# Linear attention and a gated block on one core: matmuls whose results are not read, loads moved between periods, a sum moved to PSUM, and another order of the last output steps

## The chip, the core and the metric

The kernel runs on one core of a Trainium2 chip. The metric is the device time of one execution in microseconds (us). The engines are TensorE (PE in the profile; PEld is its weight load), VectorE (DVE), ScalarE (ACT), GpSimd (POOL) and SyncE (SP), whose queue issues every DMA here. SBUF is the on-chip memory, PSUM the memory that matmuls write.

## The reference

Attention over 4 batches, 8 heads, 768 steps, head dimension 48 keeps a 48 x 48 state for each head; its result, 4 x 768 x 384, goes through a gated block with width 1024.

```python
for t in range(S):                       # attention
    cur = einsum('bhd,bhe->bhde', u * k[t], v[t])
    y[t] = einsum('bhd,bhde->bhe', r[t], state + cur)
    state = w * state + einsum('bhd,bhe->bhde', k[t], v[t])

h = maximum(x @ w_in, 0)                 # x: y with the heads side by side
u, v = h[..., :512], h[..., 512:]
v_n = (v - mean(v)) / sqrt(var(v) + 1e-6)
v_s = einsum('ts,bsd->btd', w_spatial, v_n) + b_spatial[:, None]
out = (u * v_s) @ w_out
```

## The kernel before

The attention works in 24 chunks of 128 steps (6 for each batch), the block behind it in steps of matmuls. Matmul operands are split in a high part (rounded) and a low part (the rest), and each product is three matmuls (`mm3`, L392 to L394).

A loop over `i` from -1 to 23 writes the program, and every engine does its instructions in the order written. One pass, a period, has: the results of chunk `i` (`g2`, L336, then `fin`: ScalarE casts them to `xh`, L366); the first products of chunk `i+1` (`g1`: L287 the scores, L296 the state's update); for the first seven chunks `fin_low`, where TensorE subtracts `xh` from the results in PSUM (L376) and ScalarE copies the rest to `xl` (L377); then `mid(i+1)`: VectorE merges the scores (L310), ScalarE copies the state into two block matrices (L303, L304), and VectorE makes the next state, `t1 + ub_` (L325) times the decay `w128` (L326). After that SP issues the loads of chunk `i+3` (L91 `rk`, L95 `rkv`), and chunk `i+2` is prepared (`prep`): `scale` (L248 on GpSimd, L249 on VectorE), two products with `r` and one with `k` on GpSimd (L254, L255, L258), a sum on VectorE (L261) and the diagonal on GpSimd (L270). Between the parts stand pieces of splitting the weights (`pour`: L183 to L203 for the input and output weights; L214 to L219 for the first three pieces of the spatial weights, where TensorE copies a piece to PSUM, L214, ScalarE makes the high part, L215, TensorE subtracts it, L218, and ScalarE copies the low part, L219; L172 and L173 for the other nine) and the block's steps: `moe_v` (L392 to L394 into L406, statistics L413 to L430, norm L436, L438, L443), `moe_u` (L462 to L468), `moe_sp` (L392 to L394, then L479 adds the bias on VectorE, L480 multiplies with `u` on GpSimd, and a step later `split` makes `gt`, L172 and L173) and `moe_out` (L392 to L394 with `wo_h` and `wo_l`, copy L492 to `ob`, DMA L493). `ob` has two buffers. `moe_*` steps write to `pm`, a pool of four PSUM banks that the splits use too.

The loads of the weights stand at the end of a period: six pieces of the spatial weights and the bias after period 0, four pieces of the output weights after period 2, two more spatial pieces after period 3.

Of the kernel before, what the change touches and what calls it, by code (L numbers as in the profile page):

```python
# [7 lines left out]
F32 = mybir.dt.float32  # L8
# [3 lines left out]
ALU = mybir.AluOpType  # L12
AX = mybir.AxisListType

B, H, S, D = 4, 8, 768, 48
# [3 lines left out]
P = 128  # L19
# [4 lines left out]
NP = H // 2  # L24
NK = DM // P
NS = S // P
ND = DH // P
TH = S // 2
# [8 lines left out]
def fused_kernel(ctx, tc, rkT, rkvN, wT, uB, w_in, w_sp, b_sp, w_out, out):  # L37
# [4 lines left out]
    KPOOL, DACT, VPOOL = 8, 0, 1  # L42
    XPE, SPE = 7, 3
    SIX, LAST = 6, 1
    FIRST = [0, 1, 2, 2, 5, 10]
    POUR = [(3, 4), (2, 4), (6, 4), (1, 4), (5, 4), (1, 3), (1, 5), (0, 12), (1, 13), (0, 8)]
    const = ctx.enter_context(tc.tile_pool(name="const", bufs=1))
# [23 lines left out]
    def raw_out(k):  # L71
        t = sm.tile([P, 2 * DM], U32, name="raw", tag="gt", bufs=5)
        raws["out", k] = t.rearrange("p (n k) -> p n k", k=2)
        src = w_out[k * P:(k + 1) * P, :]
        nc.sync.dma_start(out=raws["out", k], in_=src.bitcast(U32).rearrange("p (n k) -> p n k", k=2))
# [133 lines left out]
    def sp_pieces(t, j):  # L209
        def f():  # L210
            if t * NS + j < SPE:
                hi, lo = (w[:, j, t * TH:(t + 1) * TH] for w in (ws_h, ws_l))
                pm = ps_m.tile([P, 512], F32, name="pm")[:, 0:TH]
                nc.tensor.matmul(pm, eye, raws["sp", t, j], start=True, stop=False)  # L214
                nc.scalar.copy(hi, raws["sp", t, j])  # L215

                def rest():
                    nc.tensor.matmul(pm, neg, hi, start=False, stop=True)  # L218
                    nc.scalar.copy(lo, pm)  # L219

                rests.append(rest)
                if len(rests) > 1:
                    rests.pop(0)()
                if j == NS - 1 or t * NS + j == SPE - 1:
                    rests.pop(0)()
                return
            split(ws_h[:, j, t * TH:(t + 1) * TH], ws_l[:, j, t * TH:(t + 1) * TH], raws["sp", t, j])
            if t and j + 2 < NS:
                raw_sp(t, j + 2)
        return [f]  # L230
# [45 lines left out]

    SUBS = ((0, 64, 0), (1, 0, 64))

    def g1(m):
        t = at[m]  # L280
        ps = ps_a.tile([P, 2, 512], F32, name="ps")
        t["ps"] = ps
        for p in range(NP):
            for j in range(2):
                for z, s0, t0 in SUBS:
                    hd = slice(64 * j, 64 * j + 64)
                    nc.tensor.matmul(ps[s0:s0 + 64, j, p * HC:(p + 1) * HC], t["k"][hd, p, s0:s0 + 64],  # L287
                                     t["r"][hd, p, t0:t0 + 64], start=True, stop=True, skip_group_check=True)
        for p in range(NP):
            for j in range(2):  # L290
                for z, s0, t0 in SUBS:
                    if z == 1 and m % NC == NC - 1:
                        continue
                    h = 2 * p + j
                    e0 = 0 if j == 0 else 16
                    nc.tensor.matmul(ps[64 * j:64 * j + 64, s0 // 64, 256 + p * D:256 + (p + 1) * D],  # L296
                                     t["kn"][s0:s0 + 64, h * D:h * D + 64], t["v"][s0:s0 + 64, h, e0:e0 + D],
                                     start=True, stop=True, skip_group_check=True)
# [7 lines left out]
    def mid(m):  # L306
        t, c = at[m], m % NC
        ps = t["ps"]
        ua, ub_ = (ps[:, i, 256:256 + NP * D].rearrange("p (n e) -> p n e", n=NP) for i in (1, 0))
        nc.vector.copy_predicated(out=t["a"], mask=mask_u.unsqueeze(1).unsqueeze(1).to_broadcast([P, 2, NP, HC]),  # L310
                                  data=ps[:, :, 0:256].rearrange("s j (p t) -> s j p t", p=NP))
        if c == 0:
            block(sblk[1], ua)
            t1 = ua
        else:
            block(sblk[0], st["s"])
            t1 = sm.tile([P, NP, D], F32, name="t1", bufs=1)
            nc.vector.tensor_tensor(out=t1, in0=st["s"], in1=ua, op=ALU.add)
            block(sblk[1], t1)
        if c < NC - 1:  # L320
            if c == 0:
                t1 = sm.tile([P, NP, D], F32, name="t1", bufs=1)
                nc.vector.tensor_copy(out=t1, in_=ua)
            s2 = sm.tile([P, NP, D], F32, name="s2")
            nc.vector.tensor_tensor(out=s2, in0=t1, in1=ub_, op=ALU.add)  # L325
            nc.vector.tensor_tensor(out=s2, in0=s2, in1=w128.unsqueeze(2).to_broadcast([P, NP, D]), op=ALU.mult)  # L326
            st["s"] = s2

    def g2(m):
# [61 lines left out]
    def mm3(o, lh, ll, rh, rl, first, last):  # L391
        nc.tensor.matmul(o, lh, rh, start=first, stop=False)  # L392
        nc.tensor.matmul(o, lh, rl, start=False, stop=False)  # L393
        nc.tensor.matmul(o, ll, rh, start=False, stop=last)  # L394
# [76 lines left out]
    def moe_sp(b, t, d):  # L471
        ds_ = slice(d * P, (d + 1) * P)
        ts_ = slice(t * TH, (t + 1) * TH)
        pm = ps_m.tile([P, 512], F32, name="pm")
        for s, vn in enumerate(vst[b]):
            mm3(pm[:, 0:TH], vn[:, 0, ds_], vn[:, 1, ds_], ws_h[:, s, ts_], ws_l[:, s, ts_], s == 0, s == NS - 1)
        u = us.pop((b, t, d))
        g = sm.tile([P, TH], F32, name="g", bufs=2)
        nc.vector.tensor_tensor(out=g, in0=pm[:, 0:TH], in1=bb[:, ts_], op=ALU.add)  # L479
        nc.gpsimd.tensor_tensor(out=g, in0=g, in1=u, op=ALU.mult)  # L480
        gt = sm.tile([P, 2, TH], F32R, name="gt", tag="gt", bufs=5)
        gs[b, t, d] = gt
        later(1, lambda: split(gt[:, 0], gt[:, 1], g))

    def moe_out(b, t, i):
        pm = ps_m.tile([P, 512], F32, name="pm")
        o = slice(i * P, (i + 1) * P)
        for d in range(ND):
            gt = gs[b, t, d]
            mm3(pm[:, 0:DM], gt[:, 0, o], gt[:, 1, o], wo_h[:, d, :], wo_l[:, d, :], d == 0, d == ND - 1)  # L490
        ob = sm.tile([P, DM], F32, name="ob", tag="ob")
        nc.scalar.copy(ob, pm[:, 0:DM])  # L492
        nc.sync.dma_start(out=out[b, t * TH + i * P:t * TH + (i + 1) * P, :], in_=ob)  # L493
# [40 lines left out]
    def sp_loads(t):  # L534
        for j in range(NS if t == 0 else 2):
            raw_sp(t, j)
        if t == 0:
            nc.sync.dma_start(out=bb, in_=b_sp)

    DMAS = {0: lambda: sp_loads(0), 2: lambda: [raw_out(k) for k in range(ND)], 3: lambda: sp_loads(1)}  # L540
    done = 0
    for i in range(-1, NM):
        if i < 0:
# [9 lines left out]
        if i < NM - 1:  # L553
            g1(i + 1)
        if i >= 0:
            fin_low(i, *low)
        if i < NM - 1:
            mid(i + 1)
# [24 lines left out]
                tick()  # L583
        for f in parts:
            f()
        if i in DMAS:
            DMAS[i]()
    for _ in range(6):
        tick()

# [49 lines left out]
```

## Time and profile before

| what | value |
|---|---|
| median of 3 runs | 379.31 us (378.53 to 379.43) |
| the execution with the profile | 379.35 us, span 377.5 us |
| PE busy | 342.9 us (91%) |
| PEld busy | 314.1 us (83%) |
| DVE busy | 215.9 us (57%) |
| ACT busy | 145.3 us (38%) |
| POOL busy | 152.5 us (40%) |
| moved by DMA | 41.69 MB |

Busy time is of the whole span; the program has stages with different limits, so a stage is read by itself. In rows of instructions the columns are start and duration in us, engine, line, operation, output and inputs, shapes, and in brackets how long the engine had been idle and what ended that. "issue" there is time in which the engine waited for nothing that the profile shows. A matmul's duration reaches over the start of the next one, so costs are read from start to start.

### The profile page before, as it was taken

How to read it: one execution, taken by the hardware profiler on the slowest of the kernel's cores; microseconds unless marked ns; L12 is line 12 of the kernel's file. 1: busy time of each engine (PE TensorE's matmuls, PEld its weight loads, DVE VectorE, ACT ScalarE, POOL GpSimd, SP SyncE). 2: the span in 40 equal slices, each digit the busy share in tenths (PEclk: the TensorE clock that was granted, in tenths of full speed). 3: DMA queues.
4: the chain of work that ended last, by engine and by line, in shares of the span. 5: the costliest groups of instructions: out<-in, count | busy, mean ns of one | idle time of the engine just before them, and what ended most of it. 6: DMA issues, size and time to landing. Idle time of an engine off the chain costs nothing.

```text
span 377.5 us, 12269 instructions
## 1 busy us (share of the span) xinstructions
PE 342.9 (91%) x5459; PEld 314.1 (83%) x5459; DVE 215.9 (57%) x415; ACT 145.3 (38%) x320; POOL 152.5 (40%) x157
## 2 busy tenths in 40 slices
PE   2467669698999999999999999999999999999995
PEld 1456548597999998789899999889989998999994
DVE  6699975687855464577644445597444534443120
ACT  3033455756322333547313223647122335461212
POOL 5865745656265353421445273241563330003120
PEclk9996957989999999999999999999999999999999
DMA  7992933233303235303305314334031010000101
GB/s 260 417 387 92 322 144 130 82 129 129 129 2 129 73 129 180 120 20 133 115 2 180 110 71 152 128 104 150 5 127 65 4 44 25 0 0 2 42 21 64
DMA packets 14021, 41.69 MB, mean 110 GB/s; under 512 B 1680, under 2 KB 6416, under 8 KB 13968
## 3 DMA queue, kind: packets, MB, share of 16 engines
q1 hardware_dynamic: 13968, 40.90, 30.6%
q8 instruction: 43, 0.70, 0.8%
q14 instruction: 10, 0.08, 0.1%
HBM read 36.18 MB, written 4.72 MB: 108 GB/s over the span
## 4 chain that ended last, share of the span: by engine, by line
PE 81%; DVE 7%; DMA 3%; ACT 3%; issue 3%; POOL 2%; SPq 0%; POOLq 0%; DVEq 0%; ACTq 0%
PE pm L392 21%; PE pm L394 20%; PE pm L393 20%; PE xp L336 9%; PE ps L287 3%; PE ps L296 3%; DMA rkv<-rkvN 2%; DMA wst<-w_sp 2%; DVE rk L249 1%; PE pm L462 1%; PE pm L467 1%; PE pm L463 1%; DVE pm L199 1%; ACT vs L436 1%; DVE s L326 1%
## 5 line engine op out<-in xcount | busy, mean ns | idle before, releaser
L480 POOL TENSOR_TENSOR g<-g,u 128x384 f32<-128x384 f32 x32 | 32.5, 1016 | 118.0 <-DVE g L479 118.0
L392 PE MATMUL pm<-ws_h,vnorm 128*128 128x384 f32 x192 | 64.9, 338 | 0.0
L394 PE MATMUL pm<-ws_h,vnorm 128*128 128x384 f32 x192 | 64.2, 335 | 0.0
L393 PE MATMUL pm<-ws_l,vnorm 128*128 128x384 f32 x192 | 64.2, 334 | 0.0
L270 POOL TENSOR_TENSOR a<-diag,dg 128x512 f32<-128x512 f32 x24 | 25.4, 1059 | 86.0 <-DVE dg L261 56.1
L173 DVE TENSOR_TENSOR gt<-g,gt 128x384 fp32r<-128x384 f32 x32 | 21.0, 655 | 57.8 <-ACT gt L172 57.8
L172 ACT CAST gt<-g 128x384 fp32r<-128x384 f32 x32 | 16.4, 513 | 91.7 <-POOL g L480 91.7
L392 PEld LDWEIGHTS pm<-ws_h,vnorm 128*128 128x128 f32 x192 | 36.0, 188 | 0.3
L393 PEld LDWEIGHTS pm<-ws_l,vnorm 128*128 128x128 f32 x192 | 36.1, 188 | 0.0
L394 PEld LDWEIGHTS pm<-ws_h,vnorm 128*128 128x128 f32 x192 | 36.0, 188 | 0.0
L392 PE MATMUL pm<-wo_h,gt 128*128 128x384 f32 x96 | 33.0, 344 | 0.8 <-ACT gt L172 0.8
L394 PE MATMUL pm<-wo_h,gt 128*128 128x384 f32 x96 | 32.5, 338 | 0.4 <-issue 0.4
L393 PE MATMUL pm<-wo_l,gt 128*128 128x384 f32 x96 | 32.3, 336 | 0.0
L393 PE MATMUL pm<-wi_l,xh 128*128 128x512 f32 x72 | 29.6, 411 | 0.9 <-issue 0.9
L392 PE MATMUL pm<-wi_h,xh 128*128 128x512 f32 x72 | 30.2, 419 | 0.0
L394 PE MATMUL pm<-wi_h,xl 128*128 128x512 f32 x72 | 29.4, 408 | 0.0
L479 DVE TENSOR_TENSOR g<-pm,bb 128x384 f32<-128x384 f32 x32 | 17.7, 554 | 19.9 <-PE pm L394 19.8
L255 POOL TENSOR_TENSOR rkv<-rkv,ub 128x384 f32<-128x384 f32 x24 | 26.2, 1092 | 1.9
L336 PEld LDWEIGHTS xp<-rk,sb 128*32 128x32 f32 x1056 | 18.2, 118 | 9.8 <-issue 4.5
L413 DVE BATCH_NORM_STATS2 q<-vs 128x6 f32<-128x512 f32 x24 | 16.5, 687 | 16.6 <-ACT vs L406 16.6
L336 PE MATMUL xp<-a,rkv 64*32 64x64 f32 x1536 | 25.0, 234 | 0.0
L336 PE MATMUL xp<-rk,sb 128*32 128x64 f32 x1056 | 23.1, 234 | 2.1 <-ACT sb L303 2.1
(102 smaller groups left out, 733.7 us busy)
## 6 DMA issues: line engine op xcount, KB each, us to landing
rkv<-rkvN SPq DMA_DIRECT2D x24, 648.0 KB, 5.7
rk<-rkT SPq DMA_DIRECT2D x24, 512.0 KB, 4.1
out<-ob SPq DMA_DIRECT2D x24, 192.0 KB, 1.9
raw<-w_in SPq DMA_DIRECT2D x6, 512.0 KB, 9.9
wst<-w_sp SPq DMA_DIRECT2D x12, 192.0 KB, 6.7
raw<-w_out SPq DMA_DIRECT2D x4, 384.0 KB, 7.3
bb<-b_sp SPq DMA_DIRECT2D x1, 384.0 KB, 5.6
ub<-uB SPq DMA_DIRECT2D x1, 192.0 KB, 6.6
```

Source lines behind the costliest of these rows:

```text
L172: nc.scalar.copy(hi, src)
L173: (eng or nc.vector).tensor_tensor(out=lo, in0=src, in1=hi.bitcast(F32), op=ALU.subtract)
L255: nc.gpsimd.tensor_tensor(out=rn, in0=rn, in1=ub, op=ALU.mult)
L270: nc.gpsimd.tensor_tensor(out=a.rearrange("s j p t -> s (j p) t"), in0=diag.unsqueeze(1).to_broadcast([P, H, HC]), in1=dg.rearrange("s j p ...
L287: nc.tensor.matmul(ps[s0:s0 + 64, j, p * HC:(p + 1) * HC], t["k"][hd, p, s0:s0 + 64], t["r"][hd, p, t0:t0 + 64], start=True, stop=True, sk ...
L336: nc.tensor.matmul(xp[32 * g:32 * g + 32, z, jt * HC:(jt + 1) * HC], lhsT, rhs, start=(z, g) not in began, stop=True, skip_group_check=Tru ...
L392: nc.tensor.matmul(o, lh, rh, start=first, stop=False)
L393: nc.tensor.matmul(o, lh, rl, start=False, stop=False)
L394: nc.tensor.matmul(o, ll, rh, start=False, stop=last)
L413: nc.vector.bn_stats(out=q6[:, c % 3, :], in_=vs)
L479: nc.vector.tensor_tensor(out=g, in0=pm[:, 0:TH], in1=bb[:, ts_], op=ALU.add)
L480: nc.gpsimd.tensor_tensor(out=g, in0=g, in1=u, op=ALU.mult)
```

## The change

It has four parts. `warm` issues `n` matmuls of 384 columns with the constant `neg` as both operands into a `pm` bank that nobody reads: 12 in the first `g1` between its two halves, 6 ahead of each of the three L218, and 8, 6, 6, 8, 6 ahead of `fin_low` in periods 1, 2, 4, 5, 6. `bulk` spreads the loads: spatial pieces 0 to 2 after period 0, 3 to 5 and the bias after period 1, one piece of the output weights after each of periods 1 to 4, two spatial pieces after period 3. In `mid` the sum `t1 + ub_` is written over `ub_` in PSUM, and the product with the decay reads it there. In the last `moe_out` steps the three sums take the feature blocks 0 to 2 first, each in a bank of its own, and block 3 afterwards; for the last `moe_sp` the product with `u` is on VectorE.

```diff
+    SPREAD = 1
+    WARM_UPDATE, WARM_X = {-1: 12}, {1: 8, 2: 6, 4: 6, 5: 8, 6: 6}
...
                 def rest():
+                    warm({0: 6, 1: 6, 2: 6}, t * NS + j)
                     nc.tensor.matmul(pm, neg, hi, start=False, stop=True)
...
+    def warm(table, i):
+        n = table.get(i, 0)
+        if n:
+            pm = ps_m.tile([P, 512], F32, name="pm")
+        for k in range(n):
+            nc.tensor.matmul(pm[:, 0:TH].rearrange("p (n c) -> p n c", n=3), neg,
+                             neg.unsqueeze(1).to_broadcast([P, 3, P]), start=k == 0, stop=k == n - 1)
...
     def g1(m):
...
+        warm(WARM_UPDATE, m - 1)
         for p in range(NP):
...
-            nc.vector.tensor_tensor(out=s2, in0=t1, in1=ub_, op=ALU.add)
-            nc.vector.tensor_tensor(out=s2, in0=s2, in1=w128.unsqueeze(2).to_broadcast([P, NP, D]), op=ALU.mult)
+            nc.vector.tensor_tensor(out=ub_, in0=t1, in1=ub_, op=ALU.add)
+            nc.vector.tensor_tensor(out=s2, in0=ub_, in1=w128.unsqueeze(2).to_broadcast([P, NP, D]), op=ALU.mult)
...
-        nc.gpsimd.tensor_tensor(out=g, in0=g, in1=u, op=ALU.mult)
+        (nc.vector if (b, t, d) == (B - 1, 1, ND - 1) else nc.gpsimd).tensor_tensor(out=g, in0=g, in1=u, op=ALU.mult)
...
     def moe_out(b, t, i):
+        if (b, t) == (B - 1, 1):
+            if i == 0:
+                pms = [ps_m.tile([P, 512], F32, name="pm") for _ in range(3)]
+                for d0, d1 in ((0, ND - 1), (ND - 1, ND)):
+                    for k in range(3):
+                        out_sum(b, t, k, pms[k], d0, d1)
+                        if d1 == ND:
+                            out_end(b, t, k, pms[k])
+            return
         pm = ps_m.tile([P, 512], F32, name="pm")
+        out_sum(b, t, i, pm, 0, ND)
+        out_end(b, t, i, pm)
+
+    def out_sum(b, t, i, pm, d0, d1):
         o = slice(i * P, (i + 1) * P)
-        for d in range(ND):
+        for d in range(d0, d1):
...
+    def out_end(b, t, i, pm):
         ob = sm.tile([P, DM], F32, name="ob", tag="ob")
         nc.scalar.copy(ob, pm[:, 0:DM])
...
-    DMAS = {0: lambda: sp_loads(0), 2: lambda: [raw_out(k) for k in range(ND)], 3: lambda: sp_loads(1)}
+    def bulk(i):
+        if SPREAD:
+            if i in (0, 1):
+                for j in range(3 * i, 3 * i + 3):
+                    raw_sp(0, j)
+            if i == 1:
+                nc.sync.dma_start(out=bb, in_=b_sp)
+            if i in (1, 2, 3, 4):
+                raw_out(i - 1)
+            if i == 3:
+                sp_loads(1)
...
         if i >= 0:
+            warm(WARM_X, i)
             fin_low(i, *low)
...
-        if i in DMAS:
-            DMAS[i]()
+        bulk(i)
```

Line numbers of the kernel after are higher: L214 and L218 become L216 and L221, L287 and L296 become L299 and L309, L336 is L349, L376 is L389, L392 to L394 are L405 to L407; L288 is the new matmul.

TensorE's queue around the subtraction of the first spatial pieces, in period 3, before (`wst` is a piece as loaded, `ws_h` its high part, `eye` the unit matrix):

```order
L376 MATMUL xp<-xh,neg 128x192 x2
L214 MATMUL pm<-wst,eye 128x384 x2
L218 MATMUL pm<-ws_h,neg 128x384
L214 MATMUL pm<-wst,eye 128x384
L218 MATMUL pm<-ws_h,neg 128x384 x2
L336 MATMUL xp<-rk,sb_163 32x64 x12
```

The same place after:

```order
L389 MATMUL xp<-xh,neg 128x192 x2
L216 MATMUL pm<-wst,eye 128x384 x2
L288 MATMUL pm<-neg 128x384 x6
L221 MATMUL pm<-ws_h,neg 128x384
L216 MATMUL pm<-wst,eye 128x384
L288 MATMUL pm<-neg 128x384 x6
L221 MATMUL pm<-ws_h,neg 128x384
L288 MATMUL pm<-neg 128x384 x6
L221 MATMUL pm<-ws_h,neg 128x384
L349 MATMUL xp<-rk,sb_163 32x64 x12
```

Six new matmuls stand ahead of each subtraction; the results of chunk 4 (L336, now L349) follow the last.

TensorE's queue behind that, at the end of period 4's `g1` and its `fin_low`, before:

```order
L336 MATMUL xp<-rk,sb_165 32x64 x12
L336 MATMUL xp<-a_159,rkv 32x64 x32
L287 MATMUL ps<-rk 64x64 x16
L296 MATMUL ps<-rkv 64x48 x8
L376 MATMUL xp<-xh,neg 128x192 x2
```

and after:

```order
L349 MATMUL xp<-a_159,rkv 32x64 x32
L299 MATMUL ps<-rk 64x64 x16
L309 MATMUL ps<-rkv 64x48 x8
L288 MATMUL pm<-neg 128x384 x6
L389 MATMUL xp<-xh,neg 128x192 x2
```

Six new ones stand between the state's update and the subtraction of `xh`.

The end of TensorE's queue, the last twelve matmuls before (`pm_5040` is the bank of the third sum; `gt_4882`, `gt_4955`, `gt_4980`, `gt_5005` are the feature blocks 0 to 3):

```order
L392 MATMUL pm_5040<-wo_h_171,gt_4882 128x384
L393 MATMUL pm_5040<-wo_l_172,gt_4882 128x384
L394 MATMUL pm_5040<-wo_h_171,gt_4882 128x384
L392 MATMUL pm_5040<-wo_h_171,gt_4955 128x384
L393 MATMUL pm_5040<-wo_l_172,gt_4955 128x384
L394 MATMUL pm_5040<-wo_h_171,gt_4955 128x384
L392 MATMUL pm_5040<-wo_h_171,gt_4980 128x384
L393 MATMUL pm_5040<-wo_l_172,gt_4980 128x384
L394 MATMUL pm_5040<-wo_h_171,gt_4980 128x384
L392 MATMUL pm_5040<-wo_h_171,gt_5005 128x384
L393 MATMUL pm_5040<-wo_l_172,gt_5005 128x384
L394 MATMUL pm_5040<-wo_h_171,gt_5005 128x384
```

and after (`pm_5081`, `pm_5082`, `pm_5083` are the three sums, `gt_5078` is block 3):

```order
L405 MATMUL pm_5083<-wo_h_171,gt_5053 128x384
L406 MATMUL pm_5083<-wo_l_172,gt_5053 128x384
L407 MATMUL pm_5083<-wo_h_171,gt_5053 128x384
L405 MATMUL pm_5081<-wo_h_171,gt_5078 128x384
L406 MATMUL pm_5081<-wo_l_172,gt_5078 128x384
L407 MATMUL pm_5081<-wo_h_171,gt_5078 128x384
L405 MATMUL pm_5082<-wo_h_171,gt_5078 128x384
L406 MATMUL pm_5082<-wo_l_172,gt_5078 128x384
L407 MATMUL pm_5082<-wo_h_171,gt_5078 128x384
L405 MATMUL pm_5083<-wo_h_171,gt_5078 128x384
L406 MATMUL pm_5083<-wo_l_172,gt_5078 128x384
L407 MATMUL pm_5083<-wo_h_171,gt_5078 128x384
```

Block 3 was the last quarter of each sum; now it is the last quarter of all three together, so the first sum ends six matmuls before the end of the queue, where it ended 24 before it.

More of the change, by code (lines that the diff above doesn't have):

```diff
@@ L538, in sp_loads @@
             nc.sync.dma_start(out=bb, in_=b_sp)
-    DMAS = {0: lambda: sp_loads(0), 2: lambda: [raw_out(k) for k in range(ND)], 3: lambda: sp_loads(1)}
+    def bulk(i):
[9 more added lines that the diff above has]
+                sp_loads(1)
+        elif i in (0, 2, 3):
+            (lambda: sp_loads(0), None, lambda: [raw_out(k) for k in range(ND)], lambda: sp_loads(1))[i]()
     done = 0
```

## The prediction

> **What bounds the kernel now.** I read the page first, then busy time by stretch, then the waits, then the instructions in order of time where a term of the sum lies. The row PEclk of the page is TensorE's granted clock in 40 slices; the stretches are start:end, length, busy time of PE, PEld, DVE, ACT and POOL, granted clock, DMA share and GB/s.
>
> ```profile
> PEclk9996957989999999999999999999999999999999
> 14.50:49.00 34.50, 24.03 (x703) 19.61 (x702) 33.57 (x55) 11.02 (x27) 21.73 (x22) 0.87 0.78 292
> 98.00:366.00 268.00, 265.70 (x3879) 250.30 (x3872) 138.21 (x272) 98.26 (x214) 92.97 (x91) 1.00 0.23 79
> ```
>
> From 98 us on TensorE is busy for 265.70 of 268.00 us at full clock; the change touches nothing there. What it can move lies before 98 us and in the last 11 us. From 14.5 to 49 us VectorE is the bound: 33.57 of 34.50 us busy, while TensorE waits for it. So a faster TensorE alone is worth nothing there, and a microsecond taken from VectorE is worth one. At 49 us the bound changes hands:
>
> ```profile
> 47.84 0.58 PE L287 MATMUL ps<-rk 64*64 64x64 f32 x11 [2.68 <-issue]
> 49.52 0.74 DVE L310 COPY_PREDICATED a<-mask,ps 128x512 f32<-128x512 uint32 x1 [0.69 <-PE ps L296]
> 55.15 0.69 PE L218 MATMUL pm<-ws_h,neg 128*128 128x384 f32 x1 [2.50 <-ACT ws_h L215]
> 55.63 1.49 PE L214 MATMUL pm<-wst,eye 128*128 128x384 f32 x2
> 57.69 1.51 PE L336 MATMUL xp<-rk,sb 128*32 128x64 f32 x48
> 61.66 0.47 PE L376 MATMUL xp<-xh,neg 128*128 128x192 f32 x2
> 62.16 0.48 ACT L377 CAST xl<-xp 128x384 fp32r<-128x384 f32 x1 [0.94 <-PE xp L376]
> ```
>
> VectorE waits once for TensorE (0.69 us), ScalarE gives the first high part, and from 55.15 to 62.16 TensorE has no pause and everybody waits for it: L377 stands first in ScalarE's queue, and the copies, casts and norms behind it follow up to 74 us. A microsecond that TensorE loses between 55 and 62 us is therefore lost.
>
> The clock changes on a grid of 3.41 us. Four of these windows:
>
> ```profile
> 26.44:29.85 3.41, 1.50 (x67) 1.21 (x64) 3.34 (x7) 0.59 (x1) 2.09 (x2) 1.00 1.02 376
> 43.50:46.92 3.42, 1.66 (x102) 1.34 (x91) 3.42 (x7) 0.22 (x1) 1.40 (x3) 1.00 1.03 398
> 57.16:60.57 3.41, 3.41 (x114) 2.64 (x113) 1.79 (x2) 1.68 (x4) 3.33 (x4) 0.50 0.10 23
> 84.46:87.88 3.42, 2.53 (x153) 2.22 (x152) 0.94 (x3) 3.36 (x8) 2.87 (x3) 1.00 0.53 162
> ```
>
> After the first two (PE busy 44% and 49%) the clock fell to 0.50, after the fourth (74%) it stayed, and the third, full at half clock, raised it. So it falls after a window that is about half idle, and rises only after a full one.
>
> **Part A: the state's sum stays in PSUM.** L326, whose tensors both lay in SBUF, now reads PSUM.
>
> ```profile
> L326 DVE TENSOR_TENSOR s<-s,w x20: 357/358/1155, 15.4 to 297.7; 128x192 f32<-128x192 f32 x20
> 15.09 1.00 POOL L255 TENSOR_TENSOR rkv<-rkv,ub 128x384 f32<-128x384 f32 x1
> 15.36 0.95 DVE L326 TENSOR_TENSOR s<-s,w 128x192 f32<-128x192 f32 x1
> 16.05 1.11 POOL L258 TENSOR_TENSOR rkv<-rkv,tn 128x384 f32<-128x384 f32 x1
> 16.23 1.48 DVE L249 TENSOR_TENSOR rk<-rk,tt 128x512 f32<-128x512 f32 x1
> 20.04 1.04 POOL L270 TENSOR_TENSOR a<-diag,dg 128x512 f32<-128x512 f32 x1 [2.88 <-DVE dg L261]
> 24.48 1.48 DVE L249 TENSOR_TENSOR rk<-rk,tt 128x512 f32<-128x512 f32 x1
> 32.20 1.49 DVE L249 TENSOR_TENSOR rk<-rk,tt 128x512 f32<-128x512 f32 x1
> ```
>
> L326 ends 0.22 us after GpSimd's L255 (16.31 against 16.09), and L249, next in the queue, ends 0.55 after GpSimd's L258 (17.71 against 17.16): each waits out a whole GpSimd instruction, and VectorE gets its turn where one ends. With 0.36 (the median) L326 ends at 15.72, L249 asks at about 15.64 and takes the turn at 16.09 that L326 has now: done at 16.64, 1.07 earlier. L258 then comes about 0.6 later; GpSimd's wait of 2.88 us covers that. The periods at 24 and 32 us have the same L249 (1.48, 1.49), and GpSimd moves along there, since its L270 waits for VectorE: 3 x 1.07 = -3.2. Bounds: 0 (L249 finds the port taken each time) and -3.2; I take -3.2, because the order of requests is that of the rows. That the sum is written to PSUM instead of SBUF I take as free.
>
> **Part B: loads over six periods.** Seven loads are issued one to three periods later; behind chunk loads on SP's queue, they wait for TensorE with these. The moved ones are first read behind L218 (55.15) or later, so 0. The last of the output weights is now ahead of chunk 8's loads on that queue; an issue is a fraction of a us, and that chunk is read a period later: 0. The pause of 2.68 us ("issue": TensorE waited for nothing in the profile) lies in a stretch with the DMA engines at 1.03; with three of four output-weight loads out of it, I expect VectorE's 0.69 to go: bounds 0 and -0.7, I take -0.7. After it, ScalarE's cast to `xh` of the same period is late next.
>
> **Part C: matmuls with unread results.** What one costs at half clock comes from two of 512 columns, 0.43 us from start to start; 384 columns make 0.32, and half of it at full clock, 0.17.
>
> ```profile
> 33.20 0.63 PE L392 MATMUL pm<-wi_h,xh 128*128 128x512 f32 x1
> 33.63 0.63 PE L393 MATMUL pm<-wi_l,xh 128*128 128x512 f32 x1
> 11.89 1.11 PE L296 MATMUL ps<-rkv 64*64 64x48 f32 x32 [3.41 <-POOL rkv L258]
> 31.33 0.74 PE L376 MATMUL xp<-xh,neg 128*128 128x192 f32 x2 [2.13 <-ACT xh L366]
> 40.27 0.47 PE L376 MATMUL xp<-xh,neg 128*128 128x192 f32 x2 [1.17 <-ACT xh L366]
> 74.11 0.66 PE L376 MATMUL xp<-xh,neg 128*128 128x192 f32 x2 [2.98 <-ACT xh L366]
> 88.35 0.47 PE L376 MATMUL xp<-xh,neg 128*128 128x192 f32 x2 [1.36 <-ACT xh L366]
> ```
>
> Five groups lie in a pause. 12 in 3.41 us: 3.84 at half clock, 0.4 late at most, and L249 then asks at 16.04, still before 16.09: 0. The 8 at 31 us (2.6 of 2.13 at half clock) and the 6 at 40 us (1.0 of 1.17 at full clock) lie where VectorE is the bound: 0; if that cover went, 0.5. The 8 at 74 us (1.4 of 2.98) and the 6 at 88 us (1.0 of 1.36) cost nothing.
>
> The first 6 ahead of L218 lie in the pause of 2.50 us. The other 12 there and the 6 ahead of L376 at 61.66 have no pause: g1 ends there without waiting, and L376 follows at once. TensorE's path from 55.15 to the start of L376 is 6.51 us now. At full clock throughout it becomes: L218 three times 0.17, L214 0.64 (half of 1.28, the 1.49 of its row less the 0.2 for its end), 12 x 0.17, then the state's matmuls, which after a full window take
>
> ```profile
> 68.27 0.88 PE L336 MATMUL xp<-rk,sb 128*32 128x64 f32 x48
> 70.50 0.63 PE L296 MATMUL ps<-rkv 64*64 64x48 f32 x32
> ```
>
> 2.23 to the start of L296 and, for its 16 here, 0.30; then 6 x 0.17: together 6.8 to 6.9, +0.4. At half clock TensorE reaches the state's matmuls after 0.48 + 1.28 + 12 x 0.32 + 2 x 0.32 = 6.2 instead of 2.54 us, unless the clock rises on the way, which needs a full window: 3.4 to 6.8 us of unbroken work. The latest gives +3.5, the middle (5.1) +2.8: 5.1, then the remaining 1.1 at half price, 2.53 and 1.04, 9.3 in all against 6.51. Ends: +0.4 and +3.5. Before 55 us the pauses ahead of 47.84 (then a wait for `xh`) and 55.15 still make windows that are about half idle, so I take half clock, less a little for the phases in which the earlier dummies have just raised it: +2.4.
>
> At 74 us, the 8 leave 1.6 idle of a window of 3.41 (53% busy), between the 49% that fell and the 74% that stayed; the clock probably stays. What follows then runs faster, but the next xh (88.35) waits on ScalarE and VectorE, whose chain starts with the cast behind L376:
>
> ```profile
> 74.81 0.48 ACT L377 CAST xl<-xp 128x384 fp32r<-128x384 f32 x1 [0.75 <-PE xp L376]
> 78.13 0.34 PE L462 MATMUL pm<-xh,wi_h 128*128 128x384 f32 x1
> ```
>
> That cast comes 0.70 after L376 here, 0.50 at 61.66: -0.2. Bounds: 0, and half of the 4.02 us from 74.11 to 78.13, -2.0.
>
> **Part D: the end.**
>
> ```profile
> 366.52 0.34 PE L392 MATMUL pm<-wo_h,gt 128*128 128x384 f32 x1
> 367.42 1.01 POOL L480 TENSOR_TENSOR g<-g,u 128x384 f32<-128x384 f32 x1 [2.09 <-DVE g L479]
> 369.02 0.44 PE L392 MATMUL pm<-wo_h,gt 128*128 128x384 f32 x1 [0.78 <-ACT gt L172]
> 369.90 0.34 PE L392 MATMUL pm<-wo_h,gt 128*128 128x384 f32 x1
> 373.89 0.34 PE L394 MATMUL pm<-wo_h,gt 128*128 128x384 f32 x1
> 374.31 0.48 ACT L492 COPY ob<-pm 128x384 f32<-128x384 f32 x1 [1.60 <-PE pm L394]
> out<-ob SPq DMA_DIRECT2D x24, 192.0 KB, 1.9
> ```
>
> 24 matmuls from 369.90 to 373.89 are 0.1735 apart; 36 without the waits end with a start at 366.52 + 35 x 0.1735 = 372.59, 1.3 us earlier. But `ob` has two buffers, and the third copy needs the first one's, whose DMA takes 1.9 us to land. The first sum now ends late: its last matmul is the 30th, at 371.55; copy at 371.97 (0.42 later, as at the end now), DMA at 372.5, landed at 374.4, and only then the third copy, 374.4 against 374.31. The gain becomes a new wait: +0.1. Bounds -1.3 and +0.1; by the rows it is the latter. The product on VectorE instead of L480 (1.01) only makes `gt` ready earlier than 371.2, where it is first wanted: 0.
>
> **The sum.** -3.2 - 0.7 + 2.4 - 0.2 + 0.1 = -1.6 on a span of 377.5, so 375.9; the execution with the profile took 379.35, 1.85 more than its span, and the median of the runs, 379.31, is the same within 0.04. Forecast: 377.7 us. About 0.3% (1.1 us) is what can be told from no change.
>
> **Rivals.** First, the clock stays full from 40 to 62 us, and part C costs +0.4: -3.6, 375.7. For it: the dummies halve several pauses; against it: the window at 43.50 fell with 51% idle. [...]
>
> Second, gains and dummies cancel: the third port turn is missed (L310 at 30 us waits for a late g1), the 0.69 stays, part C costs 2.8: -2.1 + 2.8 - 0.2 + 0.1 = +0.6, 379.9.
>
> Third, slower: VectorE's L249 still finds the port taken in each period. It needs L249 to ask after L255 has ended, 0.45 us later than I have it; the first 12 dummies at half clock already make 0.38 of that. Then A is 0: -0.7 + 2.8 - 0.2 + 0.1 = +2.0, 381.3.
>
> **Chances.** Forecast 0.38, first rival 0.20, second 0.25, third 0.17. The forecast's own range, 376.5 to 378.7, is nearly all "faster" (0.35 of 0.38): faster 0.55, same 0.28, slower 0.17. The range for 8 in 10 takes in the first two rivals and leaves out the third: 375.4 to 380.2.
>
> **What would show it.** A: L326 at 0.36 throughout, L249 under 1.2 in the first three periods, and L218 3 to 4 us earlier than 55.15. B: no wait of VectorE ahead of L310 near 46 us. C: the granted clock at 0.50 for some windows between 44 and 58 us, TensorE busy without a break from L218 to L376, 8 us or longer. D: an idle ScalarE before the last copy that ends with a DMA, and the last matmul more than 2.5 us before the last issue. I am wrong if L249 still takes 1.48, or if the clock row is full from 30 us on.

## The result and the profile after

The changed kernel takes 382.58 us in its profiled execution (span 380.8), which is also the median of 382.46, 382.58 and 385.08 us, against 379.24 for the kernel before on the same chip. A fourth run took 388.3 us, 1.5% above the fastest, counts as slow and is not in the ratio. The ratio is 1.0119, 95% interval 1.0093 to 1.0146: 1.2% slower. Forecast were 377.7 us and a gain.

First the lines that answer to those shown of before: the granted clock in 40 slices, and three stretches (start:end, length, busy time of PE, PEld, DVE, ACT and POOL, granted clock, DMA share, GB/s).

```profile
PEclk9969989999999999999999999999999999999998
14.50:49.00 34.50, 26.20 (x728) 21.03 (x729) 32.95 (x60) 13.25 (x33) 24.38 (x23) 0.87 0.83 295
49.00:62.00 13.00, 10.20 (x194) 8.57 (x194) 7.13 (x11) 5.82 (x14) 5.54 (x5) 0.94 0.30 111
98.00:366.00 268.00, 263.29 (x3878) 248.00 (x3868) 137.25 (x270) 97.82 (x213) 91.93 (x90) 1.00 0.24 79
```

The last row is the surprise. Before, TensorE was busy for 265.70 of these 268 us; now it is for 263.29, in a stretch to which the change adds nothing. The idle time there is almost all of one kind. These are TensorE's rows of the changed kernel, in order of time, that stand behind a pause ended by "issue" (nothing in the profile was waited for), the first three of nine left out:

```profile
58.95 0.37 PE L309 MATMUL ps<-rkv 64*64 64x48 f32 x5 [0.39 <-issue]
99.82 0.33 PE L309 MATMUL ps<-rkv 64*64 64x48 f32 x6 [1.34 <-issue]
119.45 0.49 PE L309 MATMUL ps<-rkv 64*64 64x48 f32 x17 [0.95 <-issue]
136.27 0.43 PE L309 MATMUL ps<-rkv 64*64 64x48 f32 x11 [0.95 <-issue]
242.12 0.56 PE L309 MATMUL ps<-rkv 64*64 64x48 f32 x21 [0.79 <-issue]
310.81 0.44 PE L309 MATMUL ps<-rkv 64*64 64x48 f32 x9 [0.68 <-issue]
```

Five stops behind 98 us, 4.71 us. The kernel before has three there, 2.30 us, at other work:

```profile
158.41 0.50 PE L393 MATMUL pm<-wi_l,xh 128*128 128x512 f32 x1 [0.87 <-issue]
180.26 0.67 PE L296 MATMUL ps<-rkv 64*64 64x48 f32 x27 [1.07 <-issue]
281.09 0.45 PE L394 MATMUL pm<-wo_h,gt 128*128 128x384 f32 x1 [0.37 <-issue]
```

What is common to them is a count. The page gives TensorE 5523 matmuls and as many weight loads, 11,046 records, and the instruction queue 43 packets of 0.70 MB in all:

```profile
q8 instruction: 43, 0.70, 0.7%
```

That is 16,384 bytes and some 257 records a packet. I counted all of TensorE's records in the traces (matmuls, weight loads, and some 65 semaphore instructions, which the busy counts leave out): in both kernels every stop that "issue" ends stands where the number of records so far is 193 or 194 more than a multiple of 256, and it ends 2.2 to 2.8 us after a packet of this queue has started. My reading, which no run tests, is that the next instructions are not there yet. Call such a place in the count a boundary. The same holds for every such stop in all fourteen traces of this case (2.2 to 2.9 us after a packet's start).

### The profile page after: what moved, and what is told of

Same layout as the page of the kernel before. It is cut to its first block, busy times and chain, and to the rows that moved or that the text cites. A ratio compares the mean times of both kernels' runs of the same rounds, so it can differ in the third digit from the quotient of the medians.

```text
span 380.8 us, 12399 instructions
## 1 busy us (share of the span) xinstructions
PE 350.3 (92%) x5523; PEld 322.3 (85%) x5523; DVE 212.9 (56%) x416; ACT 145.3 (38%) x320; POOL 153.0 (40%) x156
## 4 chain that ended last, share of the span: by engine, by line
PE 80%; DVE 7%; DMA 4%; ACT 4%; issue 3%; POOL 0%; SPq 0%; DVEq 0%; ACTq 0%; POOLq 0%
PE pm L405 21%; PE pm L406 20%; PE pm L407 20%; PE xp L349 9%; PE ps L299 3%; PE ps L309 3%; PE pm L288 2%; DMA raw<-w_out 2%; DVE rk L252 1%; DMA wst<-w_sp 1%; DMA rk<-rkT 1%; DVE pm L201 1%; DVE a L323 1%; DVE pm L197 1%; ACT vs L449 1%
## 5 line engine op out<-in xcount | busy, mean ns | idle before, releaser
L493 POOL TENSOR_TENSOR g<-g,u 128x384 f32<-128x384 f32 x31 | 31.5, 1016 | 120.4 <-DVE g L492 120.4
L405 PE MATMUL pm<-ws_h,vnorm 128*128 128x384 f32 x192 | 64.9, 338 | 0.0
L407 PE MATMUL pm<-ws_h,vnorm 128*128 128x384 f32 x192 | 64.3, 335 | 0.0
L174 ACT CAST gt<-g 128x384 fp32r<-128x384 f32 x32 | 16.4, 513 | 91.1 <-POOL g L493 89.1
L405 PEld LDWEIGHTS pm<-ws_h,vnorm 128*128 128x128 f32 x192 | 36.0, 188 | 0.3
L407 PEld LDWEIGHTS pm<-ws_h,vnorm 128*128 128x128 f32 x192 | 36.0, 188 | 0.0
L405 PE MATMUL pm<-wo_h,gt 128*128 128x384 f32 x96 | 32.9, 343 | 0.0
L407 PE MATMUL pm<-wo_h,gt 128*128 128x384 f32 x96 | 32.3, 336 | 0.0
L405 PE MATMUL pm<-wi_h,xh 128*128 128x512 f32 x72 | 28.9, 401 | 0.0
L407 PE MATMUL pm<-wi_h,xl 128*128 128x512 f32 x72 | 28.8, 400 | 0.1
L406 PE MATMUL pm<-wi_l,xh 128*128 128x512 f32 x72 | 28.8, 400 | 0.0
L258 POOL TENSOR_TENSOR rkv<-rkv,ub 128x384 f32<-128x384 f32 x24 | 26.1, 1086 | 1.9
L309 PE MATMUL ps<-rkv 64*64 64x48 f32 x704 | 18.1, 222 | 9.3 <-issue 9.3
L261 POOL TENSOR_TENSOR rkv<-rkv,tn 128x384 f32<-128x384 f32 x24 | 26.4, 1100 | 0.0
L257 POOL TENSOR_TENSOR rkv<-rkv 128x384 f32<-128x384 f32 x24 | 24.3, 1011 | 1.7 <-DMA rkv<-rkvN 1.7
```

Of the source, the lines that this page charges most:

```text
L257: nc.gpsimd.tensor_tensor(out=rn, in0=rn, in1=kn, op=ALU.mult)
L258: nc.gpsimd.tensor_tensor(out=rn, in0=rn, in1=ub, op=ALU.mult)
L261: nc.gpsimd.tensor_tensor(out=kn, in0=kn, in1=tn_f, op=ALU.mult)
L493: (nc.vector if (b, t, d) == (B - 1, 1, ND - 1) else nc.gpsimd).tensor_tensor(out=g, in0=g, in1=u, op=ALU.mult)
```

## The ledger

How much later than in the kernel before the same instruction starts (worked out from the start times in the traces; the rows are the mask's copy into `a` of six chunks, L377's cast of period 4 at 62.16 us, and the last copy into `ob`; `ndr_128` is no_dummies_rep_128):

| start before | changed | no_dummies | sum_alone | rep_128 | rep_256 | ndr_128 | sum_172 | after_44 |
|---|---|---|---|---|---|---|---|---|
| 49.52 | -3.11 | -2.94 | -2.97 | -0.70 | +0.07 | -4.25 | -2.28 | -3.16 |
| 62.16 | -1.37 | -2.62 | -2.36 | -0.31 | +0.09 | -4.30 | -2.37 | -0.45 |
| 87.14 | -0.38 | -2.06 | -2.31 | +0.29 | +0.07 | -2.91 | -2.37 | +0.27 |
| 98.45 | +1.82 | -2.40 | -3.04 | +1.08 | +0.10 | -2.26 | -2.44 | +0.88 |
| 132.86 | +3.88 | -2.40 | -3.02 | +3.40 | +0.10 | -0.50 | -2.37 | +0.92 |
| 215.49 | +1.81 | -2.67 | -3.82 | +1.44 | -0.14 | -2.59 | -4.34 | -1.20 |
| 308.28 | +3.08 | -3.16 | -3.71 | +3.07 | -0.49 | -0.43 | -5.01 | -1.87 |
| 374.31 | +3.22 | -3.03 | -3.71 | +3.08 | -0.49 | +1.01 | -5.15 | -1.85 |

The changed kernel is ahead until 87 us, loses at each stop of its own (98, 118, 135, 241, 310 us), and gains where the kernel before has one (157, 179, 280 us). The other columns are the experiments.

## The experiments

Theory 1 says that the count sets the stops. Its rivals are the loads, and the additional matmuls by their own time. Each ratio is against the kernel before, run on the same chip, with its 95% interval.

**no_dummies: the change without its matmuls with unread results.**

```diff
-    WARM_UPDATE, WARM_X = {-1: 12}, {1: 8, 2: 6, 4: 6, 5: 8, 6: 6}
+    WARM_UPDATE, WARM_X = {}, {}
...
-                    warm({0: 6, 1: 6, 2: 6}, t * NS + j)
```

> The change without its 64 matmuls with unread results (192 of them counted with their loads would be wrong: 64 matmuls and 64 weight loads); the sum in PSUM, the spread loads and the new end stay. Theory 1, the count: TensorE's long stops ('issue') stand in both kernels where the number of its matmuls and weight loads so far is 193 more than a multiple of 256, next to a 16,384-byte packet of the instruction queue; the 128 additional instructions moved them into denser work, which cost 2.9 us behind 98 us. Without them the stops behind 98 us lie at 157, 179 and 280 us again as before the change (2.3 us instead of 4.7), and the 1.5 us of dummies between 52 and 62 us are saved: about 378 us. Theory 2, the loads: the spread loads cost the time, by a late spatial piece at 82 us and output weights at 92 us, and the stops are chance: 381 us. Theory 3, the dummies' own time alone: 1.5 us less, 381 us, with the stops of the changed kernel where they are.

Measured: 376.35 us, ratio 0.9937 (0.9924 to 0.9949). Stops at 155.2 (0.80) and 176.7 us (0.91), the work of 157 and 179 before; the one at 280 is gone, and TensorE is busy for 266.30 of the 268 us. Theories 2 and 3 had 381, theory 1 had 378, so that more was gained than any of them said. The 64 matmuls and their 64 weight loads are 128 records; since their time and their count went together here, this run alone doesn't part the two.

**pad_128 and pad_256: small matmuls at the very start.**

```diff
+        for _ in range(64 if p == 0 else 0):
+            nc.tensor.matmul(pt[0:64, 0:64], eye[0:64, 0:64], eye[0:64, 0:64], start=True, stop=True, skip_group_check=True)
         nc.tensor.transpose(pt[:, 0:P], tt[:, p, :], eye)
```

(128 in pad_256.)

> The kernel before with 64 small matmuls (64x64, and 64 weight loads) at the very start, in the 5.28 us in which TensorE has nothing to do; their result is overwritten. Nothing else moves. Theory 1, the count: every later instruction has a number 128 higher, so the stops lie where the changed kernel had them behind 98 us (near 98, 116, 132, 239 and 308 us) and no longer at 157, 179 and 280 us: 2.9 us more there, by the steps read between the two traces; what happens before 98 us, where VectorE covers part of it, is open by 1 us: 382 us (381 to 383). Theories 2 and 3: matmuls in an idle stretch cost nothing: 379.3, and the stops stay at 157, 179 and 280 us.

> The kernel before with 128 such small matmuls at the start, 256 instructions with their loads: one whole packet. Theory 1: all stops lie at the same work as before the change (157, 179, 280 us), only one packet later in the count: 379.3, within 0.4, though twice as much was added as in the run with 64. If instead additional instructions cost by their number: twice the loss of that run, 384 to 385 us. If nothing depends on the count: 379.3 in both.

Measured: 385.55 us (1.0181, 1.0167 to 1.0195) and 399.3 us (1.0536, 1.0521 to 1.0550). Both expectations missed, for two errors of mine. Such a matmul on f32 is two matmuls and two loads in the trace, so 64 of them are 256 records, a whole packet. And these, all into one corner of one tile, take 0.11 us for each matmul of the trace, where those of L287 take 0.035 (1.13 us for 32), so that they delayed the start; why they are slower is open. TensorE's first row of pad_128:

```profile
1.46 13.91 PE L146 MATMUL pm<-eye 64*64 64x64 f32 x128 [1.46 <-POOL eye L130]
```

The stops lie at 164.3 and 185.6 us (pad_128) and 178.1 and 199.4 (pad_256), the work of 157 and 179 us before, as whole packets let it be; the times tell nothing about the theories.

**rep_128 and rep_256: the first group issued three times, or five times,** in the pause that TensorE has behind it.

```diff
-        for p in range(NP):
+        for p in list(range(NP)) * (3 if m == 0 else 1):
```

(5 in rep_256.)

> The kernel before; the 16 matmuls of the first group g1(0) are issued three times instead of once, into the same tile with the same values, in the 3.41 us in which TensorE then waits for GpSimd. A group is 64 records of TensorE (32 matmuls, 32 weight loads) and takes 1.13 us, so 128 records and some 1.3 to 2.3 us of hidden work are added; everything behind it is as before, with a count higher by 128. (The 64 matmuls of the run with 128 were 256 records, one packet, and hid nothing: they delayed the start.) Theory 1, the count: the stops at 157, 179 and 280 us go, and stops appear near 98, 116, 132, 239 and 308 us, the work at which the changed kernel had them: +2.9 us behind 98 us, and before 98 us the 2.68 us at 45 us moves to about 38 us, where VectorE covers it; 380.5 to 382.5. Theory 2, the added work itself counts and not its number: 379.3, stops as before.

> The same with the first group issued five times: 256 records more, a whole packet, some 2.5 us of work in the pause of 3.41 us. Theory 1: the stops lie at the same work as before the change (157, 179, 280 us): 378.7 to 379.5, less than with half as many added. Theory 2 (added work counts): at least the loss of the run with 128.

Measured: 382.73 us, 1.0093 (1.0068 to 1.0117), with 128 records more, and 377.99 us, 0.9976 (0.9962 to 0.9990), with 256. 128 records cost 0.9%, 3.5 us; twice as many cost nothing. (382.73 is just above the range of theory 1, 377.99 just below it.) The stops of rep_128 behind 98 us are five, at the work named beforehand:

```profile
99.09 0.33 PE L296 MATMUL ps<-rkv 64*64 64x48 f32 x6 [0.56 <-issue]
118.74 0.45 PE L296 MATMUL ps<-rkv 64*64 64x48 f32 x17 [0.95 <-issue]
135.80 0.43 PE L296 MATMUL ps<-rkv 64*64 64x48 f32 x11 [1.22 <-issue]
242.18 0.55 PE L296 MATMUL ps<-rkv 64*64 64x48 f32 x20 [1.23 <-issue]
310.80 0.43 PE L296 MATMUL ps<-rkv 64*64 64x48 f32 x8 [0.62 <-issue]
```

They are the changed kernel's, to the count of matmuls left in the group (6, 17, 11, 20 or 21, 8 or 9). The counts themselves can be read from stretches that begin at 0 and end inside a stop: first the changed kernel up to its stops at 119 and 135 us, then rep_128 up to its own.

```profile
0.00:119.00 119.00, 96.18 (x1874) 83.00 (x1874) 84.75 (x164) 48.87 (x111) 68.19 (x73) 0.94 0.51 179
0.00:135.80 135.80, 112.04 (x2128) 98.25 (x2128) 92.77 (x179) 54.79 (x126) 75.52 (x80) 0.95 0.49 170
```

```profile
0.00:118.30 118.30, 88.58 (x1874) 75.69 (x1875) 89.66 (x164) 48.64 (x111) 66.23 (x73) 0.94 0.50 180
0.00:135.20 135.20, 104.42 (x2128) 90.91 (x2129) 97.83 (x179) 54.69 (x126) 73.51 (x80) 0.95 0.48 172
```

PE and PEld together: 3748 and 4256 in the one, 3749 and 4257 in the other; with four semaphore instructions between the two stops the 508 make 512, two packets. And the stop at 179 us, in the kernel before and then in rep_256:

```profile
0.00:179.50 179.50, 150.04 (x2892) 131.96 (x2893) 125.21 (x238) 76.65 (x172) 90.61 (x97) 0.93 0.45 158
```

```profile
0.00:179.50 179.50, 152.64 (x3020) 134.72 (x3021) 126.39 (x238) 76.74 (x172) 90.28 (x97) 0.90 0.44 159
```

5785 and 6041: the same time, the same work, 256 records more. rep_128's gap to the kernel before has the changed kernel's size from 133 us to the end (+3.07 and +3.08 at 308 us): what the changed kernel had won in part A and lost by the time of its own matmuls about cancelled there, and the count makes the difference that is left.

**no_dummies_rep_128: the count of the changed kernel without its matmuls** (the edits of no_dummies and rep_128). The two counts agree only behind 88 us, where the last six of the 64 stand; at 62 us the changed kernel is still 28 records short.

> The change without its 64 matmuls with unread results, and with 128 records added by the repeated first group instead: the count behind 62 us is that of the changed kernel, its time on TensorE behind 12 us is not. Theory 1: the stops near 98, 116, 132, 239 and 308 us are back, 2 to 3 us more than without them: 378.5 to 379.5; what then is missing to the changed kernel's 382.5, some 3 us, is what the dummies cost by their own time. Theory 2 (the dummies cost by their time alone): 376.4 as without them.

Measured: 379.20 us, 1.0009 (0.9991 to 1.0027), by the ratios 0.7% (2.7 us) more than no_dummies. The five stops are back (94.5, 114.4, 130.9, 236.9, 306.1 us). The changed kernel is slower still: by 1.1% (4.2 us) of the ratios, and in the traces by 4.4 us at 133 us. That is what its own matmuls cost, but not by their time alone. At 49.52 us 1.1 us of it are there already, and there the counts differ: the changed kernel has had stops at 21, 27 and 37 us, this run has none ahead of 94 us. Against no_dummies the changed kernel is level at 49.52 (0.17 us ahead), 1.25 us later at 62.16, and 1.7 at 87.14, of which 0.39 is its stop at 58.95; ahead of the stop at 98 us it is 2.6 us later. So the unread matmuls cost some 2 to 3 us by time ahead of 98 us; behind it the stops last 3.0 us longer (4.71 against 1.70 us).

The stop at 306 us costs this run more than its length. Here are the window in which it lies and the next one, in the columns of the stretches above:

```profile
304.79:308.21 3.42, 2.17 (x86) 1.90 (x74) 0.92 (x2) 1.07 (x3) 0.00 (x0) 1.00 0.17 58
308.21:311.62 3.41, 3.41 (x12) 3.36 (x11) 0.61 (x2) 0.70 (x2) 0.00 (x0) 0.50 0.02 5
```

Behind a window in which TensorE was busy for 63%, with this one stop of 1.25 us, the clock fell to half for 3.41 us. In the kernel before, the changed one, no_dummies, rep_128, rep_256, few_36, sum_alone, after_44 and sum_172_end3 the granted clock from 98 to 366 us is 1.00, with all their stops there.

**one_block: the changed kernel with the loads where they were.**

```diff
-    SPREAD = 1
+    SPREAD = 0
```

> The changed kernel with the loads where they were (a block each behind periods 0, 2 and 3), dummies, sum and end as changed. If the spread loads cost 1.6 us by what comes late (a spatial piece at 82 us by 1.1, output weights at 92 us by 0.65): about 381. If they brought VectorE's 0.69 at 46 us and cost nothing, as the prediction has it: 383.2. The count of TensorE's instructions is that of the changed kernel, so the stops behind 98 us stay.

Measured: 384.27 us, 1.0137 (1.0108 to 1.0166), against 1.0119 (1.0093 to 1.0146) with the loads spread: no difference that can be told. In its trace the mask's copy of 49.52 comes 0.36 us earlier than before, with the spread loads 3.11; of these 2.75 us 1.2 are left at 87 us, 0.4 at 98 and 1.1 at 308.

**sum_alone: the kernel before with the state's sum in PSUM, and nothing else.**

```diff
-            nc.vector.tensor_tensor(out=s2, in0=t1, in1=ub_, op=ALU.add)
-            nc.vector.tensor_tensor(out=s2, in0=s2, in1=w128.unsqueeze(2).to_broadcast([P, NP, D]), op=ALU.mult)
+            nc.vector.tensor_tensor(out=ub_, in0=t1, in1=ub_, op=ALU.add)
+            nc.vector.tensor_tensor(out=s2, in0=ub_, in1=w128.unsqueeze(2).to_broadcast([P, NP, D]), op=ALU.mult)
```

> The kernel before with the state's sum in PSUM alone (no dummies, loads and end as before). The number of TensorE's instructions is that of before. By the prediction's part A, as far as the changed kernel bore it out (the first reduction of a spatial piece at 52.37 instead of 55.15 us): 2.8 us less, 376.5 us, with the stops at the same counts as before. Rival: VectorE's gain ends at a stop of TensorE (before, 2.68 us at 45 us) or at ScalarE, and less than 1 us is left: 378.5.

Measured: 375.54 us, 0.9917 (0.9902 to 0.9932). The first L218, at 55.15 before, comes 2.64 us earlier, and in both kernels TensorE waits there for ScalarE's high part:

```profile
52.51 0.69 PE L218 MATMUL pm<-ws_h,neg 128*128 128x384 f32 x1 [4.58 <-ACT ws_h L215]
```

**few_36, sum_172, after_44: the count chosen.** From the stops of the traces so far I took a rule: at each boundary TensorE stands for 3.6 us less the time that its 304 records ahead of it took. Then 9, 43 (with the sum in PSUM) or 11 (in the changed kernel) matmuls of the first group are issued once more, ahead of it:

```diff
+        for n in range(9 if m == 0 else 0):
+            p, j, (z, s0, t0) = n // 4 % NP, n // 2 % 2, SUBS[n % 2]
+            hd = slice(64 * j, 64 * j + 64)
+            nc.tensor.matmul(ps[s0:s0 + 64, j, p * HC:(p + 1) * HC], t["k"][hd, p, s0:s0 + 64],
+                             t["r"][hd, p, t0:t0 + 64], start=True, stop=True, skip_group_check=True)
```

> The kernel before with nine matmuls of the first group g1(0) issued once more ahead of it (36 records of TensorE, 0.4 us of work in its pause of 3.41 us). From the traces so far the stops follow a rule: a boundary lies at every count of 193 more than a multiple of 256, and TensorE stands there for 3.6 us less the time that its 304 records ahead of the boundary took. Worked out by that on the trace of before with every boundary 36 records earlier in the work: stops of 1.1 to 1.3 us each near 157, 227, 261, 279 and 295 us, one near 87 us where TensorE waits for xh in any case; 7.7 us by the rule behind 75 us instead of 2.6, so 379.0 + 4 to 5 = 383 to 384 us, for nine small matmuls in a pause. Theory 2, the added work itself: 379.0.

Measured: 383.3 us, 1.0121 (1.0100 to 1.0142): nine matmuls of 0.4 us in a pause cost as much as the whole change. The stops are at the six places named (shifted by the stops ahead of them); two of the rows:

```profile
228.48 0.37 PE L301 MATMUL ps<-rkv 64*64 64x48 f32 x5 [1.17 <-issue]
...
300.10 0.33 PE L301 MATMUL ps<-rkv 64*64 64x48 f32 x7 [0.98 <-issue]
```

> The state's sum in PSUM alone (375.5 in its run), and 43 matmuls of the first group once more ahead of it (172 records, 1.7 us in the pause of 3.41 us): the number at which the rule gives the least, stops of 0.6 us near 95 and 196 us and 1.1 near 46 us, 1.1 us behind 75 us instead of 2.6. Theory 1: 374.1 (373.5 to 374.8). Theory 2: 375.5 or, if the added 1.7 us of work cost, more.

Measured: 373.38 us, 0.9866 (0.9847 to 0.9886), 0.5% below sum_alone. Of the two stops of 0.6 us, 0.25 and 0.28 are there; the one of 1.1 near 46 us is 2.75.

> The changed kernel with eleven matmuls of the first group once more (44 records more; 172 with its 128). By the rule, stops of 0.6 us near 98 us and 0.7 near 202 us are left of those near 59, 98, 118, 135, 241 and 310 us (6.3 us by the rule behind 75 us become 1.3; 4.7 us of stops behind 92 us in the trace). The dummies' own cost of some 2 us ahead of 90 us stays. Theory 1: 4 us less than the changed kernel, 378.5 (377.5 to 379.5), with nothing taken out of it. Theory 2 (the dummies, the loads or the end cost the time themselves): 382.5 or more.

Measured: 378.46 us, 1.0003 (0.9983 to 1.0023): with 44 more records, the changed kernel is level with the kernel before. One stop of 0.24 us is left behind 92 us, and TensorE is busy for 267.76 of the 268 us from 98 us on. Nothing was taken out: moving the stops alone is worth the 1.2%. That doesn't make the rest of the change free. The kernel before still has its 2.30 us of stops behind 98 us, this one has 0.24; at the same count behind 88 us, sum_172, which has the sum in PSUM and nothing else of the change, takes 0.9866. In the traces it leads by 3.3 us at 98 us and by 3.1 at 308: what the unread matmuls and the moved loads cost beside the stops behind 98 us.

**sum_172_end3: the best version,** sum_172 with the change's new end and `ob` with three buffers. The spatial pieces loaded last (`wst`) share these buffers, so they have three as well.

```diff
-            w = sm.tile([P, TH], F32, name="wst", tag="ob")
+            w = sm.tile([P, TH], F32, name="wst", tag="ob", bufs=3)
...
-        ob = sm.tile([P, DM], F32, name="ob", tag="ob")
+        ob = sm.tile([P, DM], F32, name="ob", tag="ob", bufs=3)
```

> As sum_172, with the new end (last output steps by feature block, the last product on VectorE) and three buffers for ob instead of two. By part D of the prediction the new end gains TensorE 1.3 us and loses it in the third copy, which waits for the first one's DMA (1.48 us of ScalarE in the changed kernel). Without that wait: 1.3 to 1.4 us less than sum_172, 372.7. Rival: the copies and the issues at the end queue anyway, and less than 0.5 us is left: 373.6.

Measured: 372.22 us, 0.9840 (0.9819 to 0.9861). Here is the end on ScalarE, of the changed kernel and then of this one:

```profile
375.05 1.00 ACT L520 COPY ob<-pm 128x384 f32<-128x384 f32 x2 [3.54 <-PE pm L407]
377.52 0.48 ACT L520 COPY ob<-pm 128x384 f32<-128x384 f32 x1 [1.48 <-DMA out<-ob]
```

```profile
365.60 1.52 ACT L512 COPY ob<-pm 128x384 f32<-128x384 f32 x3 [3.49 <-PE pm L399]
```

The third copy no longer waits 1.48 us for the first one's DMA. The medians of sum_172 and this version differ by 1.16 us, but their intervals overlap; the traces are clearer: from the copy that starts at 355.25 us in the kernel before to the last one, this version gains 1.30 us and sum_172 none. This version is 1.6% faster than the kernel before and 2.8% faster than the changed one (0.9840 by 1.0119).

## Why the prediction was wrong

**The step that failed** is a sentence ahead of the sum: that from 98 us on "the change touches nothing there". Part C costed 64 matmuls by their time and by the pauses that take them in. That 128 records also move every later boundary was no term at all; rep_128 and no_dummies_rep_128 show its size, +3.5 and +2.7 us. The other terms about hold in their sum: part A -3.2 (sum_alone), the unread matmuls 2 to 3 us by time against +2.2 forecast, part D +0.1, and only part B's -0.7 brought nothing that can be told. The failure was to be seen: three rows with "issue" stood in the trace of before behind 98 us, and its 2.30 us of idle time there were taken as fixed.

**Part A was right.** L339 takes 0.36 throughout, and in the first and third period L252 ends 0.55 us behind the end of GpSimd's L258 (L255 before), at 16.78 and 31.61 us; in the second it ends 0.55 us behind that of L261 (L258 before), at 24.91, and takes 1.32, not under 1.2. The first L218 (now L221) comes 2.8 us earlier, not 3 to 4. That VectorE waits for a port is the prediction's reading; the rows show the times alone:

```profile
L339 DVE TENSOR_TENSOR s<-ps,w x20: 356/357/357, 15.7 to 299.9; 128x192 f32<-128x192 f32 x20
16.01 0.77 DVE L252 TENSOR_TENSOR rk<-rk,tt 128x512 f32<-128x512 f32 x1
23.59 1.32 DVE L252 TENSOR_TENSOR rk<-rk,tt 128x512 f32<-128x512 f32 x1
30.83 0.78 DVE L252 TENSOR_TENSOR rk<-rk,tt 128x512 f32<-128x512 f32 x1
```

Forecast -3.2, and alone it measures 378.75 - 375.54 = 3.2 us. The size is partly luck: 2.4 us are won by 62 us, the rest comes when the stops and waits behind shrink.

**Part B** put the wait of VectorE down to the wrong cause. It is gone ahead of L323, as forecast:

```profile
46.40 0.72 DVE L323 COPY_PREDICATED a<-mask,ps 128x512 f32<-128x512 uint32 x1
```

But the pause of 2.68 us, which I put down to the loads, was one of the stops, and VectorE's wait came from it. sum_alone and rep_128, with the loads where they were, have no wait ahead of this copy either: the stop is 0.72 us in the one and gone in the other. The loads lengthen the stop: one_block has 2.48 us there, the changed kernel, at the same count, none.

That the moved loads cost 0 isn't settled. ScalarE's L174 waits 2.18 us for the last spatial piece, which takes 4.3 us to land instead of 2.3; in the kernel before (second row, L172) the wait is 0.17 us:

```profile
81.37 0.51 ACT L174 CAST ws_h<-wst 128x384 fp32r<-128x384 f32 x1 [2.18 <-DMA wst<-w_sp]
80.96 0.51 ACT L172 CAST ws_h<-wst 128x384 fp32r<-128x384 f32 x1 [0.17 <-DMA wst<-w_sp]
```

With the loads moved no_dummies has 1.79 us there, without it one_block has 0.22, but rep_128 1.55. TensorE's L475 then waits for the low part of an output weight:

```profile
86.77 0.75 DVE L323 COPY_PREDICATED a<-mask,ps 128x512 f32<-128x512 uint32 x1 [2.64 <-PE ps L309]
92.24 0.45 PE L475 MATMUL pm<-xh,wi_h 128*128 128x384 f32 x1 [0.65 <-DVE wo_l L205]
```

No load is late here: the last output weights were issued at 72.24 us and took 3.2 us to land, and VectorE has no pause from 86.77 us to its L205. It is late since it waited for TensorE's L309. On the whole the gain and whatever the moved loads cost cancel, as far as one_block can tell.

**Part C** had about the right size by another way than it said, which is luck. Between 27 and 74 us the clock is at half only from 47.12 to 50.53 us, nearer to the first rival than to the forecast. From the first L221 to L389 TensorE takes 8.0 us instead of 6.5, +1.5 and not +2.4, of which 0.39 is a stop. The rest of the 2 to 3 us comes between 62 and 98 us, in waits for ScalarE and VectorE such as the 0.65 us of L475. The six at 88 us cost nothing directly, as forecast: L389 starts 0.05 us after the cast to `xh` ends, as in the kernel before and in no_dummies.

```profile
86.54 1.31 PE L288 MATMUL pm<-neg 128*128 128x384 f32 x6
87.40 0.48 ACT L379 CAST xh<-xp 128x384 fp32r<-128x384 f32 x1
87.93 0.47 PE L389 MATMUL xp<-xh,neg 128*128 128x192 f32 x2
```

But the eight at 74 us did not keep the clock up: it fell behind a window 57% busy. Two windows with the one that follows each:

```profile
50.53:53.95 3.42, 1.58 (x7) 1.32 (x8) 1.78 (x3) 2.40 (x5) 0.84 (x1) 1.00 0.00 0
53.95:57.36 3.41, 3.41 (x123) 3.08 (x122) 0.51 (x1) 1.78 (x4) 3.33 (x4) 1.00 0.02 5
71.01:74.43 3.42, 1.96 (x10) 1.11 (x9) 2.38 (x5) 2.79 (x7) 3.34 (x4) 1.00 0.46 144
74.43:77.84 3.41, 3.41 (x11) 2.93 (x10) 3.34 (x7) 1.38 (x3) 1.78 (x3) 0.50 0.89 259
```

With 46% the clock stayed, with 57% it fell, and in no_dummies_rep_128 with 63%; it rose at 50.53 us behind a window in which TensorE was busy for 2.84 of 3.41 us (83%). So the prediction's reading, that a window about half idle brings it down and only a full one raises it, does not hold as a rule on one window's share. The longest gap in 71.01:74.43 is the 1.37 us ahead of L389. What decides stays open; no run here tests it.

**Part D was right to the tenth:** last copy +0.14 us against its place at 308 us (+3.22 and +3.08), forecast +0.1, by the wait named. With the third buffer the 1.3 us came (1.30 in the traces).

**The rivals** that I priced had 381.3 us as the slowest, with part A at 0; the loss came with part A intact, from a cause that was in none of them. So the range failed too.

## What to carry to other kernels

Read where the idle time marked "issue" of the bound engine lies, and count that engine's instructions up to each stop: if the counts agree modulo some number (256 here), every addition or removal of instructions ahead moves the stops, and a variant must be compared at more than one such offset before its own merit is judged. Here the offset alone was worth from 378 to 383 us; a few matmuls in an early pause set it to a better value, once the rest of the kernel is fixed (43 in the kernel with the sum in PSUM were worth 0.5%). Work placed in a pause is free by its time only if the pause is still there after the rest of the change.

## What the runs showed of the hardware

In the traces of the kernel before and of the changed one the instruction queue moved 43 packets of 16,384 bytes each, and from stop to stop the count of TensorE's records goes up by multiples of 256 (or one more or less). Behind 75 us the fourteen traces have 478 boundaries, and the time of the 304 records ahead tells where TensorE stops (worked out from the start times). At all 45 stops these records took 2.3 to 3.2 us (2.43, 2.73 and 3.18 in the kernel before), and the next one came 3.2 to 4.0 us after the first of them, a stop of 0.2 to 1.3 us. At the 433 other boundaries they took 3.1 us or more. Ahead of 75 us, where the DMA engines are busy with loads (a share of 0.78 from 14.5 to 49 us before, 0.83 after), TensorE stops at slower work too (6.2 us for the 304 records ahead of the stop at 47.84 us in the kernel before) and for longer, up to 2.9 us (18 to 21 us in the changed kernel, with a DMA share of 1.02). In sum_172_end3, with the boundaries placed by the count, stops of 0.20 us in all are left behind 98 us, and TensorE is busy for 267.80 of the 268 us. That TensorE waits for the packet itself is read from the times of the packets, and no run tests it; the runs show that the stops go with the count. Why the boundaries lie at 193 is open.
